# Two raw weight pieces in a free F buffer, and six conversion steps dealt earlier, in a kernel of a recurrent attention and a hardswish layer

## The chip, the cores and the metric

The kernel runs on one core of one Trainium2 chip. The metric is the device time of one execution in microseconds; the time before is the median of three runs. The engines are called PE (TensorE), DVE (VectorE), ACT (ScalarE), POOL (GpSimd) and SP (SyncE, which here only issues DMAs).

## The reference

Four batches of eight heads go through a recurrence of 768 steps with a state of 40 x 40 for each head; its output, 3072 rows of 320, goes through two dense layers with a hardswish between them. The inputs of the recurrence are float32. The two weights, 320 x 2048 and 2048 x 320, come as float64.

```python
for t in range(S):
    kt, vt, rt = (k[:, :, t], v[:, :, t], r[:, :, t])
    wt, at, bt = (w[:, :, t], a[:, :, t], b[:, :, t])
    y[:, :, t] = np.einsum('bhd,bhde->bhe', rt, state)
    Sa = np.einsum('bhde,bhe->bhd', state, at)
    state_decay = state * wt[:, :, None, :] - np.einsum('bhd,bhe->bhde', Sa, bt)
    state = state_decay + np.einsum('bhd,bhe->bhde', vt, kt)
x = y.transpose(0, 2, 1, 3).reshape(B * S, H * D)
h = x @ w_in
g = h * np.clip(h + 3.0, 0.0, 6.0) / 6.0
return (g @ w_out).astype(np.float32)
```

## The kernel before, in words

**Units.** The sequence is cut into chunks of 64 steps. A unit is two batches over one chunk (128 partitions), a group is four units (NU), and there are six groups, 24 units. For each unit `prepare` makes what doesn't depend on the state, in stages named W, gam, A, B, F, K, factor, E and EV. Within a chunk the recurrence is a triangular system; `invert` solves it for the four units of a group at once, from the tile F that the units' F stages have filled, and `third_block` (called X and Y in the plan for the first group) finishes it. `step` then does what depends on the state, in stages RT, VT, C, R, U, UT, S, rS, sn, H, y, move and move2. Most stages put matmuls into a PSUM tile that rotates over a few buffers (`ps_pair`), and then take the result out with DVE or ACT: y writes yg (L977, for the first two units) or ys (L980, which POOL then turns into yg, L981); sn adds to the state (L954); C, E and H take a masked score (L517); UT, S, RT, VT and rS are taken out by ACT (L917, L880, L831, L864, L933). The stages move and move2 send yg to xt, the input of the dense layers, by eight DMAs on SP (L995, L1000); move2 fills the third slot of xt, which only the narrow last part of the features uses.

**Dense layers.** `feed_forward` yields matmuls in small pieces: `expand` makes h (L1051), takes it out by a relu on ACT (L1066) and a multiply on DVE (L1067) into gt, and `contract` multiplies gt by wout (L1092). `pieces(n)` puts n of them into the order. The two PSUM buffers of h are shared by successive jobs. The first job takes unit 0, the second unit 1.

**Weights.** The float64 weights are loaded raw, as pairs of 32-bit words, in 20 pieces of 512 KB, and converted on the chip. `load_weights` is a generator: each `next` is one step, and a piece takes four of them. The first masks the high words into `parts` (DVE, L349) and turns the exponent into a factor by two ACT instructions (L350, L352); the second multiplies the piece before (DVE, L360); the third and fourth make the mantissa (DVE, L369 and L373). Raw pieces need a home in SBUF, and `raw_homes` names one for each piece: a to h are parts of a tile `raw` with tag F (a, b), of wout and win (c to f) and of tinv (g, h); "x", "fb" and "tt" are buffers of `invert`. `free` gives the piece that must have been converted before a home may be filled again. A load (DMA on SP, L327) is issued as soon as its home is free and `limit` lets it; `limit` is 13 at first and 20 after the fourth line of the plan. Tag F has two buffers: F of the first group is in one, `raw` in the other.

**Order.** The schedule is manual: each engine runs its instructions in the order in which the program records them, SP its DMAs too. The second half of the first group's work follows a plan written out by hand. An entry such as 3UT:10 runs stage UT of unit 3 and deals 10 conversion steps between its matmuls and what takes their result out. A part of the plan:

```python
0sn:2 0H:1 Y:2
1U 1UT:2 0y
2RT:1 Y:1
1sn:1 1H:1 2VT:2 0move 0move2
1y:2 2R
2S:3 3RT:2
1move 1move2 2U:3 2UT:1 2C:5
3R:4 3VT
2rS:3 2sn:3 2H:4 3S:2
2y:3 3U:1 3UT:10 3C:5
```

With the last of these lines the second group begins: its W is transposed (L471) into `one` and `pair`, ACT copies it out (L534, L538), and DVE runs the scans L541 and L552. Its WA tile, with tag x, is loaded before that.

Of the kernel before, what the change touches and what calls it, by code (L numbers as in the profile page):

```python
# [8 lines left out]
F32 = mybir.dt.float32  # L9
I32 = mybir.dt.int32  # L10
U32 = mybir.dt.uint32
# [5 lines left out]
P = 128  # L17
BL = 64
# [12 lines left out]
def kernel(  # L31
# [50 lines left out]
    NH = NU * H  # L82
# [8 lines left out]
    inv = ctx.enter_context(tc.tile_pool(name="inv", bufs=1))  # L91
# [129 lines left out]
    for i in range(3):  # L221
        t = const.tile([P, H, BL], F32, name=f"score{i}")
# [14 lines left out]
    for p in range(NP):  # L237
        t = const.tile([P, 2, NPR, SLOT], F32, name=f"state{p}")
        nc.vector.memset(t[:], 0.0)
        state.append(t)  # L240
        t = const.tile([P, 2, NPR], F32, name=f"last{p}")
# [16 lines left out]
    for i, (x, y) in enumerate([(0, DFF // 2), (0, NJ // 2)]):  # L258
        for n, z in enumerate((x, y)):
            t = win[:, :, z:z + H * SLOT] if i == 0 else \  # L260
                wout[:, z:z + 4, :].rearrange("p j m -> p (j m)")[:, 0:2 * H * SLOT].rearrange(
                    "p (n x) -> p n x", n=2)
            t = t.rearrange("p n (h e) -> p n h e", e=SLOT)
            name = ("WA", "BK")[i][n]
# [3 lines left out]
    for u in range(2):  # L268
        t = win2[:, u * NPR * P:(u + 1) * NPR * P]
        placed["rgam", 2 + u] = t.rearrange("p (r t) -> p r t", t=P)  # L270
    WC = 256
# [5 lines left out]
    def raw_homes():  # L277


        raws = inv.tile([P, NH, BL], F32, name="raw", tag="F", bufs=2)  # L280
        raws = raws[:].rearrange("p h t -> p (h t)").bitcast(U32)
        places = [raws[:, n * 4 * WC:(n + 1) * 4 * WC] for n in range(2)]
        for j in (NJ // 4, 3 * NJ // 4):
            places.append(wout[:, j:j + NJ // 4, :].rearrange("p j m -> p (j m)")[:, 0:4 * WC].bitcast(U32))
        places = [x.rearrange("p (n c t) -> p n c t", n=2, t=2) for x in places]
        for c in (DFF // 4, 3 * DFF // 4):
            x = win[:, :, c:c + 2 * WC].bitcast(U32)
            places.append(x.rearrange("p n (c t) -> p n c t", t=2))
        x = tinv[:].rearrange("p h t -> p (h t)").bitcast(U32)
        for n in range(2):  # L290
            y = x[:, n * 4 * WC:(n + 1) * 4 * WC]
            places.append(y.rearrange("p (n c t) -> p n c t", n=2, t=2))
        a, b, c, d, e, f, g, h = places
        order = [g, h, a, b, c, d, e, f, a, b, c, d, "x", "fb", "tt", a, b, "fb", "tt", a]
        free = [None] * 8 + [2, 3, 4, 5, None, None, None, 8, 9, 13, 14, 15]
        left = {}
        for n, (x, before) in enumerate(zip(order, free)):
            if isinstance(x, str):
                if x not in left:
                    left[x] = inv.tile([P, L, L], F32, name=f"raw_{x}", tag=x)  # L300
                x = left[x][:].rearrange("p t s -> p (t s)").bitcast(U32)
                x = x.rearrange("p (n c t) -> p n c t", n=2, t=2)
            yield x, before

    def load_weights():
# [3 lines left out]


        todo, homes = weight_pieces(), raw_homes()
        loaded, done, issued = deque(), [], [0]
        upcoming = []
# [843 lines left out]
    third, F, group_F = [], None, []  # L1157
# [65 lines left out]
    n, cleared = 0, []  # L1223
# [19 lines left out]
    def block(i, j):  # L1243

        if i % NU < 2:
            if j == 0:
# [5 lines left out]

    PLAN = """X X:2 0U:4 0UT:2 1R
              0sn:2 0H:1 Y:2
              1U 1UT:2 0y
              2RT:1 Y:1
              1sn:1 1H:1 2VT:2 0move 0move2
              1y:2 2R
              2S:3 3RT:2
              1move 1move2 2U:3 2UT:1 2C:5  # L1260
# [193 lines left out]
```

## Time and profile before

| what | value |
|---|---|
| median of 3 runs | 799.37 us (797.8 to 799.43) |
| profiled execution | 800.17 us |
| its span | 798.4 us, mean granted clock 0.956 |
| 70 to 80 us | PE busy 9.62, DVE 6.63, ACT 8.51 of 10 us |
| 110 to 120 us | PE busy 6.25, DVE 7.19, ACT 4.79 of 10 us |
| 120 to 130 us | PE busy 8.07, DVE 9.64, ACT 4.76 of 10 us |
| 200 to 210 us | PE busy 9.93, DVE 7.44, ACT 6.07 of 10 us |

The span runs from the first to the last instruction of the program; the time of an execution has a little around it. Times inside the profile are counted from the start of the span. A row of a timeline gives start, length, engine, source line, operation, the tile written and those read, shapes and the count of equal instructions in a row, and in brackets how long the engine had been idle before it and what ended that. Line numbers are those of the kernel before.

### The profile page before, as it was taken

To read this page: it belongs to the slowest core of one execution; us is meant where nothing else is said; L and a number is where in the kernel's file an instruction comes from. 1 tells how busy PE (TensorE), PEld (TensorE's weight loads), DVE (VectorE), ACT (ScalarE), POOL (GpSimd) and SP (SyncE) were. 2 spreads that over 40 slices of the span, in tenths; PEclk is the share of its full clock that TensorE was granted. 3 is DMA by queue.
4 is the path that set the end of the run, shared out by engine and by line. 5 is a ranking of instruction groups with operands and counts; after the bars stand their busy time and mean duration, and the time that the engine had idled before them with its cause. 6 is when DMAs were issued, how large, how long until landed. Compare 5 with 4: busy or idle time off the path is not lost.

```text
span 798.4 us, 35296 instructions
## 1 busy us (share of the span) xinstructions
PE 734.0 (92%) x15832; PEld 624.0 (78%) x15832; DVE 500.5 (63%) x986; ACT 307.1 (38%) x648; POOL 177.1 (22%) x318
## 2 busy tenths in 40 slices
PE   5726778999999989999999999999999999999998
PEld 4625667878778878788888888888888888888886
DVE  7898877689546699445798355888444983323210
ACT  2337653222553424452334454334444324412111
POOL 6403012421223313123214123304222202000000
PEclk9855798999999999999999999999999999999999
DMA  9693653420324322233212223213222101110000
GB/s 122 113 202 87 155 140 55 78 46 9 57 51 72 62 44 39 44 62 59 45 40 42 49 54 63 50 30 62 40 51 45 24 16 29 30 25 13 14 19 17
DMA packets 174214, 45.02 MB, mean 56 GB/s; under 512 B 157424, under 2 KB 172784, under 8 KB 174064
## 3 DMA queue, kind: packets, MB, share of 16 engines
q1 hardware_dynamic: 169760, 42.03, 27.8%
q8 instruction: 125, 2.05, 1.1%
q10 hardware_dynamic: 4304, 0.74, 0.7%
q14 instruction: 25, 0.20, 0.1%
HBM read 34.08 MB, written 3.93 MB: 48 GB/s over the span
## 4 chain that ended last, share of the span: by engine, by line
PE 77%; DVE 8%; issue 5%; SPq 5%; DMA 3%; ACT 1%; POOL 1%; POOLq 0%; DVEq 0%; ACTq 0%
PE h L1051 27%; PE o L1092 23%; PE pair L509 4%; PE pair L969 3%; SPq L455 3%; PE one L471 2%; PE pair L946 2%; PE pair L481 2%; PE pair L853 2%; PE pair L891 2%; PE pair L687 1%; PE pair L911 1%; PE pair L927 1%; PE one L875 1%; SPq L452 1%
## 5 line engine op out<-in xcount | busy, mean ns | idle before, releaser
L1051 PE MATMUL h<-xt,win 128*128 128x128 f32 (+1 forms) x2304 | 252.6, 284 | 3.2 <-DVE gt L1067 2.7
L1051 PEld LDWEIGHTS h<-xt,win 128*128 128x128 f32 (+1 forms) x2304 | 232.9, 193 | 20.6 <-issue 5.4
L1092 PE MATMUL o<-wout,gt 128*128 128x320 f32 x768 | 230.2, 443 | 0.0
L1092 PEld LDWEIGHTS o<-wout,gt 128*128 128x128 f32 x768 | 138.3, 190 | 50.2
L1067 DVE SCALAR_TENSOR_TENSOR gt<-gt,h 128x512 f32<-128x512 f32 x96 | 62.0, 682 | 71.2 <-ACT gt L1066 71.0
L1066 ACT ACTIVATE gt<-h,three 128x512 f32<-128x512 f32 x96 | 62.2, 686 | 101.6 <-PE h L1051 101.2
L981 POOL TENSOR_TENSOR yg<-ys,gam 128x512 f32<-128x512 f32 x22 | 39.7, 1803 | 162.6 <-DVE ys L980 71.8
L738 DVE TENSOR_TENSOR prod<-x 128x30 f32<-128x30 f32 (+9 forms) x180 | 67.2, 373 | 8.8 <-POOL x L723 3.3
L660 POOL TENSOR_TENSOR KBt<-K,rgt 128x320 f32<-128x320 f32 x22 | 19.1, 866 | 212.3 <-ACT rgt L649 207.4
L744 DVE TENSOR_TENSOR x<-x,prod 128x30 f32<-128x30 f32 (+9 forms) x180 | 62.3, 346 | 5.4
L954 DVE TENSOR_TENSOR state<-pair,state 40x320 f32<-40x320 f32 (+1 forms) x44 | 21.4, 487 | 65.5 <-PE pair L946 39.2
L517 DVE COPY_PREDICATED score<-mask,pair 128x512 f32<-128x512 int32 x71 | 50.0, 723 | 1.7 <-PE pair L509 1.2
L980 DVE TENSOR_TENSOR ys<-pair,ys 128x512 f32<-128x512 f32 x22 | 15.2, 690 | 40.9 <-PE pair L687 21.7
L552 DVE TENSOR_TENSOR_SCAN wm<-wm,start 128x528 f32<-128x528 f32 x24 | 37.6, 1566 | 0.8
L541 DVE TENSOR_TENSOR_SCAN prods<-wm,start 128x528 f32<-128x528 f32 x24 | 30.1, 1260 | 10.2 <-ACT wm L538 10.1
L831 ACT ACTIVATE RT<-pair 128x512 f32<-128x512 f32 x21 | 12.5, 597 | 52.8 <-PE pair L481 52.7
L692 ACT ACTIVATE EV<-pair 64x320 f32<-64x320 f32 x44 | 19.0, 432 | 33.7 <-PE pair L687 23.1
L806 ACT ACTIVATE tinv<-pair 32x256 f32<-32x256 f32 x48 | 18.0, 375 | 30.1 <-PE pair L796 29.4
L569 POOL COPY gam<-prods 128x256 f32<-128x256 f32 x24 | 22.5, 938 | 30.6 <-DVE prods L541 26.7
L1110 ACT ACTIVATE ob<-o 128x320 f32<-128x320 f32 x22 | 9.6, 435 | 49.4 <-PE o L1092 29.6
L969 PE MATMUL pair<-score,KBt 64*64 64x64 f32 x1472 | 27.4, 221 | 1.1 <-DVE state L954 0.9
L969 PEld LDWEIGHTS pair<-score,KBt 64*64 64x64 f32 x1472 | 24.0, 134 | 3.7 <-DVE state L954 1.4
(262 smaller groups left out, 1061.6 us busy)
## 6 DMA issues: line engine op xcount, KB each, us to landing
V<-in_v_dram SPq DMA_DIRECT2D x96, 40.0 KB
out_dram<-ob SPq DMA_DIRECT2D x47, 80.0 KB
R<-in_r_dram SPq DMA_DIRECT2D x92, 40.0 KB
B<-in_b_dram SPq DMA_DIRECT2D x42, 80.0 KB
K<-in_k_dram SPq DMA_DIRECT2D x42, 80.0 KB
W<-in_w_dram SPq DMA_DIRECT2D x37, 80.0 KB
A<-in_a_dram SPq DMA_DIRECT2D x37, 80.0 KB
xt<-yg SPq DMA_DIRECT2D x72, 40.0 KB
```

The source lines that it names most:

```text
L509: nc.tensor.matmul(out=o[i][half(q), n, :], lhsT=lhs[half(i, D), n ^ (2 * q * swap), half(q)], rhs=rhs[half(i, D), n, half(q)], start=True ...
L517: nc.vector.copy_predicated(out=x[:].rearrange("p (i h) t -> p i h t", i=2), mask=mask8, data=o[2])
L541: nc.vector.tensor_tensor_scan(out=prods[:].rearrange("p r m i -> p (r m i)"), data0=wm[:, 0:SCAN], data1=start[:], initial=0.0, op0=ALU.m ...
L552: nc.vector.tensor_tensor_scan(out=back, data0=back, data1=start[:], initial=0.0, op0=ALU.mult, op1=ALU.add)
L738: nc.vector.tensor_tensor(out=pv, in0=_ap(x[:], (i + 1) * L + i, [[L, n], [0, i]]), in1=_ap(x[:], i * L, [[0, n], [1, i]]), op=ALU.mult,)
L744: nc.vector.tensor_tensor(out=rest, in0=rest, in1=pv, op=ALU.add)
L969: nc.tensor.matmul(out=y[q][half(s), pr, :], lhsT=o[name][half(q), h * D:h * D + SLOT], rhs=m[name][half(q), 4 * rs + 2 * s + j, :], start ...
L981: nc.gpsimd.tensor_tensor(out=yg[:], in0=m["ys"][:].rearrange("p r q t -> p r (q t)"), in1=o["G"][:], op=ALU.mult)
L1051: nc.tensor.matmul(out=hp[c][:, i, :], lhsT=lhsT, rhs=rhs, start=(begun[c] == 0), stop=(begun[c] == 3 * NQ - 1))
L1066: nc.scalar.activation(out=gt[:], in_=hp[c][:], func=AF.Relu, bias=three[:], scale=1.0)
L1067: nc.vector.scalar_tensor_tensor(out=gt[:], in0=gt[:], scalar=6.0, in1=hp[c][:], op0=ALU.min, op1=ALU.mult)
L1092: nc.tensor.matmul(out=op[:], lhsT=gts[c][:, n, :], rhs=wout[:, c * HJ + r * NQ + n, :], start=((split or r == 0) and c == 0 and n == 0), ...
```

## The change

The 16th and 17th piece get a home of their own, a tile `more` with tag F, that is, the buffer of the first group's F, which is no longer needed then; the pieces behind them move up in the list of homes. With that, three pieces (the two in `more`, and the first in a) are issued without waiting for late conversions, and the last home is "fb". In the plan three steps are dealt behind the matmuls of y of unit 0, where there were none, and four instead of one behind those of sn of unit 1; the steps that are dealt later are thereby six steps further on. PE's order of instructions is the same as before. On SP the three loads stand ahead of the moves of unit 0; the load of the 19th piece stands behind them, and that of the last behind the moves of unit 1, ahead of WA.

```diff
-        order = [g, h, a, b, c, d, e, f, a, b, c, d, "x", "fb", "tt", a, b, "fb", "tt", a]
-        free = [None] * 8 + [2, 3, 4, 5, None, None, None, 8, 9, 13, 14, 15]
+        order = [g, h, a, b, c, d, e, f, a, b, c, d, "x", "fb", "tt", 0, 1, a, b, "fb"]
+        free = [None] * 8 + [2, 3, 4, 5, None, None, None, None, None, 8, 9, 13]
         left = {}
         for n, (x, before) in enumerate(zip(order, free)):
+            if isinstance(x, int):
+                if x == 0:
+                    more = inv.tile([P, NH, BL], F32, name="more", tag="F", bufs=2)
+                    more = more[:].rearrange("p h t -> p (h t)").bitcast(U32)
+                x = more[:, x * 4 * WC:(x + 1) * 4 * WC].rearrange("p (n c t) -> p n c t", n=2, t=2)
             if isinstance(x, str):
@@
               0sn:2 0H:1 Y:2
-              1U 1UT:2 0y
+              1U 1UT:2 0y:3
               2RT:1 Y:1
-              1sn:1 1H:1 2VT:2 0move 0move2
+              1sn:4 1H:1 2VT:2 0move 0move2
               1y:2 2R
```

## The prediction

> **What bounds the kernel now.** I read the page's busy times first, then where TensorE (PE) waits, then the stretch from 78 to 135 us on each engine's timeline, then that stretch in windows that follow the clock's own steps.
>
> ```profile
> PE 734.0 (92%) x15832; PEld 624.0 (78%) x15832; DVE 500.5 (63%) x986; ACT 307.1 (38%) x648; POOL 177.1 (22%) x318
> ```
>
> PE is the bound over the whole. In windows of 10 us it is busy for 8.6 to 10 us everywhere from 140 to 790 us, so what an early stage gains can be carried to the end, but only as PE time. The change works between 78 and 122 us, where PE waits. The timelines of DVE, ACT and PE there (start, length, row, idle time before it and its releaser):
>
> ```profile
> 79.92 0.69 DVE L977 TENSOR_TENSOR yg<-lent,gam 128x512 f32<-128x512 f32 x1 [1.97 <-PE lent L969]
> ...
> 84.91 0.49 DVE L954 TENSOR_TENSOR state<-pair,state 128x320 f32<-128x320 f32 x1 [2.62 <-PE pair L946]
> ...
> 111.14 0.43 DVE L349 TENSOR_SCALAR parts<-raw 128x512 uint32<-128x512 uint32 x1 [2.21 <-DMA raw<-in_moe_w_out_dram]
> ...
> 115.24 0.43 DVE L349 TENSOR_SCALAR parts<-raw_fb 128x512 uint32<-128x512 uint32 x1 [1.54 <-DMA raw_fb<-in_moe_w_out_dram]
> ```
>
> ```profile
> 121.25 0.58 ACT L917 ACTIVATE UT<-pair 128x512 f32<-128x512 f32 x1
> ```
>
> ```profile
> 108.39 1.16 PE L1051 MATMUL h<-xt,win 128*128 128x128 f32 x8 [2.06 <-DVE gt L1067]
> ...
> 113.16 0.69 PE L911 MATMUL pair<-tinv,RR 64*64 64x64 f32 x32 [2.07 <-DVE ys L980]
> ...
> 121.93 1.08 PE L471 MATMUL pair<-ident,WA 128*128 128x128 f32 x4 [3.60 <-issue]
> ...
> 131.41 1.34 PE L969 MATMUL pair<-score,KBt 64*64 64x64 f32 x64 [0.87 <-DVE state L954]
> ```
>
> DVE has two holes (1.97 and 2.62 us) early, and later waits twice for raw weight pieces (2.21 and 1.54). Behind those waits stand ys, and on ACT three conversion pairs (L350, L352) ahead of UT. UT ends at 121.83 and the transposes of WA, which need its PSUM pair, start at 121.93: the 3.60 us put down to "issue" are UT's. From there a full DVE (122.83, the first scan L541, to 131.3) sets y of unit 3 at 131.41. The windows (length, busy time of each engine, clock, DMA share, GB/s):
>
> ```profile
> 107.11:110.53 3.42, 2.14 (x80) 2.02 (x82) 1.49 (x3) 1.08 (x2) 0.00 (x0) 1.00 0.76 194
> 110.53:113.94 3.41, 1.34 (x92) 1.22 (x88) 2.56 (x5) 1.77 (x3) 0.70 (x1) 1.00 0.88 206
> 113.94:117.35 3.41, 3.41 (x41) 3.29 (x31) 2.07 (x5) 1.45 (x2) 0.89 (x1) 0.50 1.01 301
> ...
> 120.77:124.18 3.41, 2.25 (x11) 2.28 (x12) 3.27 (x6) 2.27 (x6) 0.04 (x1) 0.50 0.00 0
> 124.18:127.59 3.41, 3.41 (x55) 2.96 (x57) 3.28 (x6) 0.83 (x2) 3.41 (x6) 0.50 0.52 84
> ...
> 168.55:171.97 3.42, 1.97 (x68) 1.61 (x68) 3.25 (x6) 0.50 (x2) 3.09 (x5) 1.00 0.13 23
> 171.97:175.38 3.41, 3.41 (x40) 2.47 (x39) 3.24 (x10) 1.23 (x3) 0.00 (x0) 0.50 0.47 83
> ```
>
> The granted clock is 1.00 or 0.50 for a whole window. A window with 1.45 us of idle PE (168.55) or 2.07 (110.53) is followed by 0.50, one with 1.28 (107.11) is not; 0.50 ends only behind a full window (124.18, not 120.77).
>
> **The change, part by part.**
>
> *Six steps moved forward.* A piece costs DVE L349 0.42, L360 0.68, L369 0.42 and L373 0.69, 2.2 us, and ACT 0.72 + 0.72. Six steps are a piece and a half: 3.3 us of DVE. The three behind y of unit 0 (L369, L373, L349: 1.53) fit in the hole of 1.97, the three behind sn of unit 1 (L349, L360, L369: 1.52) in that of 2.62. On ACT one pair slips ahead of RT (80.51) and tinv; they end some 0.7 us later, and nothing waits for them. Cost: nothing. Were a hole gone, it would be 1.5 us each. All other DVE rows from 85 to 103 us keep their places, six steps further on.
>
> *Loads.* Pieces 16 to 18 no longer wait for a freed home and are issued behind raw_tt, at 89 us, ahead of unit 0's moves. Three issues of 0.52 put all that SP does behind them (moves, R, WA) 1.6 us later, and 1.5 MB stand ahead of the moves in the DMA queues. Before, DMA is nearly idle there (28 GB/s from 93.46 to 96.87); at the rate of 317 GB/s from 98 to 99 us the 1.5 MB take 4.7 us from about 92.3, to 97.0. PE comes to unit 0's first h at 97.17. The trace shows no landing times, so bounds: nothing, if the moves pass the loads, to 1.3 us, if they land at 98.5. I take 0.5, below the middle: the loads' last byte is due about when PE comes to h. The last three moves serve the narrow part of h alone, at 105 us. The Trainium skill, "DMA: Bandwidth & Descriptors", Queues, rings and completion order, says that an engine takes its ring's descriptors in order, which speaks against this change; without that rule the term would be 0.
>
> *A worse place on ACT.* With the pieces six steps on, ys of unit 2 (L933, before 102.19) comes behind one more pair: L349 ends at 101.7, the pair at 103.2, ys at 103.8, 1.0 later, and H waits for its PSUM. Behind state (103.2) DVE has L349, L360, L369, L373 (2.0), then the score (0.73) and the L349 of piece 18, to 106.3. Its pair (to 107.9) and S (108.4) now stand straight ahead of the relu L1066: first relu 109.05, first gt 109.7, h of unit 1 at 109.9 instead of 108.39; with the 0.5 of the moves, 110.4. PE idles 2.8 us ahead of it.
>
> *Clock there.* 2.8 us is over every idle sum above that brought 0.50, and I take 0.50: h x8 2.07 (row at 114.46) and y of unit 2 2.12 (row at 77.77) instead of 1.16 each. ys L980 starts at 114.3 instead of 112.41. At 1.00 it would be 112.7.
>
> *The tail.* Here the three DMA waits and two of three ACT pairs are gone; the last piece (raw_fb, issued near 108; the old one took 5.0 us from 110.27 to DVE's release) is there by 113. From ys (0.69): L360, L369, L373, L349, 2.0 with overlaps, to 117.0; pair to 118.5; UT to 119.1; WA transposes at 119.2 instead of 121.93. On DVE the last multiply to 119.2, the score to 119.9, first scan at 119.8: 3.0 earlier than 122.83. Scan to y of unit 3 took 8.6, so y stands at 128.4, 3.0 early.
>
> *What is late next.* PE runs from 119.2 through h, rS, sn, H and o at full clock to about 125.3 and waits 3.1 us for y, instead of 0.87. That brings 0.50 and it lasts through the rest of a window and one full one, some 5.1 us: 2.6 of PE time lost (1.7 to 3.4 for one or two whole windows), in a part where PE is then the bound. The lead of 3.0 shrinks to 0.4. "TensorE: Matmul & The Clock Gate", Why this matters for your kernels, warns of idle gaps over about 3 us; by it the 2.8 us gap would keep the clock, and the sum would be nearer to -2. The trace differs (1.45 us idle sufficed), so the row decides.
>
> **Sum.** The profiled execution took 800.17 (span 798.4 and 1.8 around it), 0.8 above the median. -3.0 + 2.6 = -0.4: 799.8 on its scale, 799.0 against the median of 799.37. A measurement of this kernel can tell about 0.2%, 1.6 us, from no change.
>
> **Rivals.** *The clock holds* at y of unit 2 or falls for one window alone at y of unit 3: the scan is 4.6 early (1.6 more) and 1.7 is given back, -2.9, or 3.0 less 1.3 or nothing: 796.4 to 797.7, say 796.5. For it: 107.11 kept 1.00 with 1.28 us idle, and a gap can be split by a window's edge. Against: two gaps near 3 us. *The moves land late*: at the 194 to 206 GB/s of 107 to 114 us the 1.5 MB take 7.5 us, to 99.8, and h starts near 100.5. PE idles 3 us more, at 0.50; state of unit 2, the relu and the whole DVE tail come 2.5 to 3.3 later, the lead of 3.0 is gone and the clock's loss stays: +2.3 (between 1.6 and 3.0), 801.7. It decides from a landing after 98.6. For it: the queue was at 0.76 to 1.01 share in those windows; against: 317 GB/s for the same kind of piece alone. *The waits only change place* (the last L349 still waits for raw_fb): it would have to land 4 us later than I reckon; the time is 799.4.
>
> **How the numbers follow.** Forecast 0.42, waits unchanged 0.03 (both within 0.2%): 0.45. Clock holds: 0.26. Moves late: 0.29. The range reaches from inside the first rival to the second's price, 797.0 to 801.8; the forecast's own range is 797.8 to 800.9.
>
> **What would show it.** Right: no DVE wait at L349 for raw or raw_fb; relu of unit 0 (106.93 before) near 109; WA transposes near 119; y of unit 3 near 128.5 behind some 3 us of idle PE; 0.50 in the window around it. Wrong: h of unit 0 later than 99 (second rival), a clock of 1.00 from 127 on with y before 129 (first), L349 waits that remain (third).

## The result, and the profile after

The changed kernel is slower. Its median is 801.42 us (797.49 to 805.62, 22 runs) against 799.21 us (796.76 to 801.13, 22 runs) for the kernel before: ratio 1.0027, 95% interval 1.0017 to 1.0038, that is 2.2 us. This is the second rival of the prediction, in its size (801.7) and in its sign; its mechanism is only a part of what happened.

The execution that was profiled took 805.42 us (span 803.7), 4.0 above its median, so the spans (803.7 and 798.4) must not be subtracted. It was also 0.92 us late before the change acts: the first yg starts at 80.84 instead of 79.92. Below, "from yg" means a time counted from the start of that row in its own profile. Line numbers of the kernels after are five higher from the list of homes on (L349 is now L354, and so on). Ratios are turned into us by 799.

The busy times of the whole span hardly differ:

```profile
PE 736.1 (92%) x15832; PEld 625.3 (78%) x15832; DVE 500.6 (62%) x986; ACT 306.9 (38%) x648; POOL 176.2 (22%) x318
```

DVE's timeline after. The holes ahead of yg and of state of unit 1 are filled, as forecast (1.97 to 0.45, 2.62 to 0.66). No masking step waits for a raw piece any more. But one conversion step behind ys takes 1.51 instead of 0.42 us:

```profile
80.84 0.69 DVE L982 TENSOR_TENSOR yg<-lent,gam 128x512 f32<-128x512 f32 x1 [0.45 <-PE lent L974]
...
85.54 0.49 DVE L959 TENSOR_TENSOR state<-pair,state 128x320 f32<-128x320 f32 x1 [0.66 <-PE pair L951]
...
117.47 0.69 DVE L985 TENSOR_TENSOR ys<-pair,ys 128x512 f32<-128x512 f32 x1 [2.11 <-PE pair L974]
118.08 0.68 DVE L365 TENSOR_TENSOR wout<-raw,parts 128x512 f32<-128x512 f32 x1
118.68 1.51 DVE L374 TENSOR_SCALAR raw<-raw 128x512 uint32<-128x512 uint32 x1
```

PE's timeline after, the rows that answer to those of before:

```profile
99.60 5.42 PE L1056 MATMUL h<-xt,win 128*128 128x128 f32 x24 [1.00 <-ACT parts L357]
...
113.41 2.08 PE L1056 MATMUL h<-xt,win 128*128 128x128 f32 x8 [3.60 <-DVE gt L1072]
...
123.35 0.63 PE L476 MATMUL pair<-ident,WA 128*128 128x128 f32 x4 [1.40 <-issue]
...
132.84 1.99 PE L974 MATMUL pair<-score,KBt 64*64 64x64 f32 x64 [3.07 <-DVE state L959]
134.75 4.50 PE L1097 MATMUL o<-wout,gt 128*128 128x320 f32 x8
```

The first h of unit 0 now waits for its input. The releaser in that row is a wrong guess: the semaphores of unit 0's first four moves are complete at 98.90, 99.10, 99.28 and 99.46 (read from the trace's semaphore updates), before 92.7 to 93.65. From yg the h is 1.5 late. 1.00 of that is this wait. The other 0.5 is PE's own delay: on ACT a conversion pair now stands ahead of RT of unit 3, which starts 14.1 from yg in place of 13.0 (ACT before, then after):

```profile
92.91 0.59 ACT L831 ACTIVATE RT<-pair 128x512 f32<-128x512 f32 x1
```

```profile
93.60 0.72 ACT L355 ACTIVATE parts<-parts,low 128x512 f32<-128x512 int32 x1 [0.36 <-DVE parts L354]
94.36 0.72 ACT L357 ACTIVATE parts<-parts,low 128x512 int32<-128x512 f32 x1
94.98 0.58 ACT L836 ACTIVATE RT<-pair 128x512 f32<-128x512 f32 x1
```

Everything behind the h is late in turn, and the clock is 0.50 where PE had waited (length, busy time of each engine, clock, DMA share, GB/s):

```profile
91.24:94.65 3.41, 1.42 (x65) 1.16 (x64) 3.24 (x8) 2.94 (x5) 0.00 (x0) 0.99 0.89 269
94.66:98.07 3.41, 2.46 (x67) 2.38 (x68) 3.34 (x8) 3.22 (x7) 0.00 (x0) 0.50 0.82 266
98.08:101.49 3.41, 2.41 (x12) 2.04 (x11) 3.38 (x7) 2.21 (x4) 0.45 (x2) 0.50 0.24 41
101.50:104.90 3.40, 3.40 (x17) 3.27 (x16) 3.08 (x7) 2.52 (x4) 0.00 (x0) 0.51 0.72 189
...
128.74:132.15 3.41, 1.03 (x4) 0.38 (x2) 3.32 (x9) 0.00 (x0) 0.91 (x4) 1.00 0.34 49
132.16:135.57 3.41, 2.73 (x66) 2.42 (x67) 1.87 (x4) 0.00 (x0) 0.00 (x0) 0.50 0.23 55
135.58:138.98 3.40, 3.40 (x8) 2.12 (x7) 0.11 (x2) 0.00 (x0) 0.00 (x0) 0.50 0.58 93
```

Where the time went, from yg, in us:

| point | before | after | difference | forecast |
|---|---|---|---|---|
| first h of unit 0 | 17.25 | 18.76 | +1.5 | +0.5 |
| state of unit 2 | 23.23 | 25.79 | +2.6 | +0.5 |
| first relu | 27.01 | 31.12 | +4.1 | +2.6 |
| ys of unit 2 | 32.49 | 36.63 | +4.1 | +1.9 |
| first scan of the second group | 42.91 | 43.42 | +0.5 | -3.0 |
| y of unit 3 | 51.49 | 52.00 | +0.5 | -3.0 |
| W's transposes behind the o matmuls | 56.96 | 60.20 | +3.2 | -0.4 |

### The profile page after: what moved, and what is told of

Read it like the earlier page. It is cut to its first block, busy times and chain, and to the rows that moved or that the text cites. A ratio compares the mean times of both kernels' runs of the same rounds, so it can differ in the third digit from the quotient of the medians.

```text
span 803.7 us, 35294 instructions
## 1 busy us (share of the span) xinstructions
PE 736.1 (92%) x15832; PEld 625.3 (78%) x15832; DVE 500.6 (62%) x986; ACT 306.9 (38%) x648; POOL 176.2 (22%) x318
## 4 chain that ended last, share of the span: by engine, by line
PE 76%; DVE 13%; issue 5%; DMA 2%; ACT 2%; POOL 1%; SPq 1%; DVEq 0%; POOLq 0%; ACTq 0%
PE h L1056 26%; PE o L1097 22%; PE pair L514 4%; PE pair L974 3%; PE pair L951 2%; PE one L476 2%; PE pair L486 2%; DVE prod L743 2%; DVE x L749 2%; DVE wm L557 2%; PE pair L896 2%; PE pair L858 1%; DVE prods L546 1%; PE pair L916 1%; PE pair L932 1%
## 5 line engine op out<-in xcount | busy, mean ns | idle before, releaser
L974 PE MATMUL pair<-score,KBt 64*64 64x64 f32 x1472 | 29.2, 230 | 4.6 <-DVE state L959 3.1
L811 ACT ACTIVATE tinv<-pair 32x256 f32<-32x256 f32 x48 | 17.9, 374 | 30.7 <-PE pair L801 30.1
```

The costliest lines, as they stand in the source:

```text
L974: nc.tensor.matmul(out=y[q][half(s), pr, :], lhsT=o[name][half(q), h * D:h * D + SLOT], rhs=m[name][half(q), 4 * rs + 2 * s + j, :], start ...
```

## The experiments

Three causes were put against each other. **L**: the loads ahead of unit 0's moves. **S**: the six steps' new place among ACT's and DVE's work. **C**: the clock, which falls behind PE's wait ahead of y of unit 3 whatever came before. Each ratio is to the kernel before on the same chip. The last column is the time from yg to W's transposes in the profiled execution; it ranks the kernels nearly as the medians do.

| kernel | ratio | 95% interval | W from yg |
|---|---|---|---|
| before | 1 | | 56.96 |
| changed | 1.0027 | 1.0017 to 1.0038 | 60.20 |
| loads_behind | 1.0006 | 0.9996 to 1.0016 | 57.66 |
| homes_only | 1.0004 | 0.9992 to 1.0016 | 58.04 |
| plan_only | 1.0052 | 1.0038 to 1.0066 | 62.17 |
| o_in_gap | 0.9980 | 0.9965 to 0.9995 | 54.35 |
| behind_and_gap | 0.9971 | 0.9960 to 0.9983 | 52.49 |
| behind_gap_pair | 0.9945 | 0.9929 to 0.9961 | 52.60 |
| before_gap | 0.9981 | 0.9970 to 0.9992 | 53.77 |
| loads_on_act | 1.0064 | 1.0052 to 1.0077 | 62.01 |
| moves_on_act | 1.0009 | 0.9995 to 1.0023 | 58.04 |
| pair_only | 0.9991 | 0.9976 to 1.0006 | 56.71 |
| behind_gap_pair_rt | 0.9943 | 0.9923 to 0.9963 | 50.74 |
| h_repeated | 1.0011 | 1.0000 to 1.0022 | 57.26 |

**Loads behind the moves** (loads_behind).

```diff
-        if t == 3:
-            limit[0] = PIECES
+        if t in (3, 4):
+            limit[0] = {3: PIECES - 5, 4: PIECES}[t]
```

> The changed kernel, with one thing put back: pieces 16 to 18 are held until unit 0's eight moves are issued. Theory L (the loads ahead of the moves are the cost): the moves are issued from 89.6 and land by 94; unit 0's first h waits for nothing and starts near 98.0 instead of 99.6; the half clock there is one window shorter; state of unit 2 near 104 instead of 106.6, first relu near 109 instead of 112.0, ys near 114.5 instead of 117.5. Median 799.0 (798.3 to 799.6), 2 to 3 below the changed kernel's 801.4. Theory S (the six steps' new place on ACT and DVE is the cost): no matter, within 0.6 of 801.4. Theory C (the clock's fall ahead of y of unit 3 takes the lead whatever comes before): 0.50 behind 132 remains in any case; under L and C together 799.0.

Measured 1.0006, 1.7 us below the changed kernel (0.5 to 2.8 with both intervals): a little less than L expects (2 to 3), and more than S allows if it were the only cause (0.6). Its PE timeline:

```profile
97.58 4.52 PE L1056 MATMUL h<-xt,win 128*128 128x128 f32 x24
...
129.26 1.99 PE L974 MATMUL pair<-score,KBt 64*64 64x64 f32 x64 [3.06 <-DVE state L959]
131.18 4.41 PE L1097 MATMUL o<-wout,gt 128*128 128x320 f32 x8
```

The moves landed by 94.5 and h waits for nothing, though from yg it is still 0.6 later than before (17.9). State of unit 2 starts at 103.77 and ys at 113.91. From yg, y of unit 3 is 1.9 ahead of before. Behind it the clock is 0.50, and W is 0.7 behind: 2.6 are given back there.

**Homes alone, plan alone** (homes_only, plan_only): one half of the change each.

```diff
 homes_only, against the changed kernel
-              1U 1UT:2 0y:3
+              1U 1UT:2 0y
-              1sn:4 1H:1 2VT:2 0move 0move2
+              1sn:1 1H:1 2VT:2 0move 0move2
 plan_only, against the changed kernel
-        order = [..., "x", "fb", "tt", 0, 1, a, b, "fb"]
-        free = [None] * 8 + [2, 3, 4, 5, None, None, None, None, None, 8, 9, 13]
+        order = [..., "x", "fb", "tt", a, b, "fb", "tt", a]
+        free = [None] * 8 + [2, 3, 4, 5, None, None, None, 8, 9, 13, 14, 15]
```

> The homes of the change with the plan of before: two loads (into more) stand ahead of unit 0's moves, the third behind them; no step is dealt earlier. Theory L: moves land near 97.6, h of unit 0 near 97.9, 0.7 late, and the half clock lasts longer there: 800.0 (799.3 to 800.7). Theory S: nothing has a new place on ACT and two waits for raw pieces go: 798.7 (798.0 to 799.3).

> The plan of the change with the homes of before: six steps dealt earlier, and only one load (16th, 512 KB) ahead of unit 0's moves. Theory L: h of unit 0 at most 0.4 late; the waits for raw pieces at the first masking step come back behind 105; 799.3 (798.7 to 800.2). Theory S: the pairs ahead of ys of unit 2 and ahead of S and relu are there as in the changed kernel, so the cost is too: 801.0 (800.4 to 801.8), first relu later than 109.

homes_only came out at 1.0004, between the two expectations and inside the range of L alone. Its h:

```profile
97.52 5.46 PE L1056 MATMUL h<-xt,win 128*128 128x128 f32 x24 [0.56 <-DMA xt<-yg]
```

Together the runs give a series. Ahead of unit 0's first four moves stand 0, 1, 2 and 3 loads of 512 KB (loads_behind, plan_only, homes_only, changed), and the last of the four is complete at 94.46, 95.95, 97.38 and 99.46, from yg at 14.8, 16.3, 17.7 and 18.6: some 1.3 us for each load. These are single executions: without the two runs that use ACT's queue, the six profiles with no load ahead of the moves have it at 13.1 to 14.8 and the four with three loads at 18.0 to 19.5, so between 1.1 and 2.1 for each. PE is ready for h at 17.1 from yg in plan_only, 17.3 in homes_only and 17.8 in the changed kernel (before 17.25). So the first load is hidden, and h waits 0.56 behind two loads and 1.00 behind three.

plan_only is the slower half, 4.2 us, more than either theory had: L had named the waits for raw pieces, but not their size. With steps six earlier but pieces that still wait for homes, DVE stands 5.15 us at a masking step, ahead of relu's multiply in its order, and PE behind that (DVE's row, then PE's):

```profile
111.70 0.43 DVE L354 TENSOR_SCALAR parts<-raw_fb 128x512 uint32<-128x512 uint32 x1 [5.15 <-DMA raw_fb<-in_moe_w_out_dram]
```

```profile
115.47 2.08 PE L1056 MATMUL h<-xt,win 128*128 128x128 f32 x8 [6.88 <-DVE gt L1072]
```

So the halves don't add (1.0004 and 1.0052 against 1.0027): the homes take away a wait that the plan makes.

**o matmuls into the gap** (o_in_gap); **both remedies** (behind_and_gap); **the same in the kernel before** (before_gap).

```diff
+        owed[0] += {BEGIN + 1: 2, BEGIN + 2: -2}.get(t, 0)
         if t >= BEGIN - 2:
             pieces(3 if t < BEGIN else 1.5 if t < BEGIN + 3 else 0)
```

> The changed kernel, with eight of the profile's o matmuls (2.4 us at full clock) moved from behind y of unit 3 to ahead of it, into the 3.07 us in which PE waits there. Theory C: idle ahead of y of unit 3 falls to 0.7, the clock stays 1.00 through 132 to 139, and the transposes of A come near 134.3 instead of 139.1; 797.0 (796.3 to 798.5). Without C, or if the lead is taken up by a full DVE later on: 801.4 (800.6 to 802.0) though the gap is filled.

> Both remedies at once: loads 16 to 18 behind unit 0's moves, and eight of the profile's o matmuls ahead of y of unit 3. If the two costs are separate they add: measured alone, the first took the ratio to before from 1.0027 to 1.0006 and the second to 0.998, so 0.996, 3.3 us under before: 3.2 below (2.2 to 4.4). First h waits for nothing, y of unit 3 near 128 behind 0.9 us of idle PE at 1.00, A's transposes near 129.5. If the gap's clock gives back whatever was gained ahead of it only in part, or the second half of the loss is one and the same cost: no better than the gap alone, 0.998.

> The kernel before with the same o matmuls ahead of y of unit 3, where PE waits only 0.87 us. Theory C: there is no fall of the clock to avoid in most executions, and 2.4 us of work stand in a gap of 0.9, so y comes 1.5 later, PE has the same work: no change, 1.000 (0.9985 to 1.0015). If the reordering as such is what helped: 0.9955, as much as it did to the changed kernel.

o_in_gap measured 0.9980, 3.8 below the changed kernel, as C expects. PE's timeline of it:

```profile
131.10 1.34 PE L974 MATMUL pair<-score,KBt 64*64 64x64 f32 x64 [0.91 <-DVE state L959]
132.37 0.66 PE L476 MATMUL one<-ident,A 128*128 128x128 f32 x4
```

Both together gave 0.9971, a little less of a gain than the sum of the two (0.9959), whose own uncertainty covers the difference. But the rival's 0.998 lies inside the interval too (up to 0.9983), so this run does not show that the two add. before_gap was a miss: 0.9981 and not 1.000. PE's wait of 0.87 is gone there and work stands in its place; this gain is no matter of the clock, and it was left out of the expectation. It is within the interval of what was measured (0.6 to 2.4 us); whether it is all of it is not shown. So o_in_gap could not settle C by itself: it mixes filled time and clock. That asked for the next run.

**H of unit 3 written four times** (h_repeated): useless work in the gap.

```diff
-            x = scores(m["UT"], m["RT"], swap=True)
+            x = scores(m["UT"], m["RT"], swap=True, times=4 if i == 3 else 1)
...
-        for n in range(NPR):
+        for n in [*range(NPR)] * times:
```

> The changed kernel with the matmuls of H of unit 3 written four times over (the same result, 1.9 us of PE work for nothing), ahead of y of unit 3, in whose 3.07 us of waiting they lie. No work is moved, so a gain can only come from the clock. Theory C: idle ahead of y of unit 3 falls to 1.2, the clock stays 1.00 behind it, y takes 1.34 instead of 1.99 and the o matmuls behind it 2.4 instead of 4.5; 2.7 below the changed kernel where the clock would have fallen, 0.9993 to before (0.9985 to 1.0008). Without C: nothing is gained, 1.0027 (1.0017 to 1.0040).

Measured 1.0011: 1.3 us less than the changed kernel, although PE does some 1.7 us more. The difference of the two ratios, 0.0016, has an interval of about 0.0015 either way, so C holds in sign, and with half of the expected size. In the profile all of it is there:

```profile
131.72 1.34 PE L974 MATMUL pair<-score,KBt 64*64 64x64 f32 x64 [0.91 <-DVE state L959]
132.99 2.42 PE L1097 MATMUL o<-wout,gt 128*128 128x320 f32 x8
```

The profiles agree without exception. In the six kernels with 3.06 or 3.07 us of waiting ahead of y of unit 3 (changed, loads_behind, plan_only, loads_on_act, moves_on_act, pair_only) the clock is 0.50 behind it and the next eight o matmuls take 4.06 to 4.54. In the eight with at most 0.92 it is 1.00; where the eight still stand there (before, homes_only, h_repeated) they take 2.42.

**The pair out of relu's way** (pair_only; behind_gap_pair and behind_gap_pair_rt, both with the loads behind and the o matmuls in the gap as well). The first two deal two steps behind y of unit 2 in place of behind S of unit 3; the third also moves a masking step behind the scaling of the state, so that its pair no longer stands ahead of RT of unit 3.

```diff
-              2rS:3 2sn:3 2H:4 3S:2
-              2y:3 3U:1 3UT:10 3C:5
+              2rS:3 2sn:3 2H:4 3S
+              2y:5 3U:1 3UT:10 3C:5
 only in behind_gap_pair_rt
-              2S:3 3RT:2
-              1move 1move2 2U:3 2UT:1 2C:5
+              2S:3 3RT:1
+              1move 1move2 2U:4 2UT:1 2C:5
```

> The changed kernel with the one masking step and multiply moved from behind S of unit 3 to behind y of unit 2, loads and o where the change has them. Theory S (1.5 to 1.8 us of the loss are the pair ahead of S and relu): relu near 110.3 instead of 112.0, 1.5 below the changed kernel, 1.0008 to before (1.0000 to 1.0018). If the gap ahead of y of unit 3 takes it back: y of unit 3 earlier by 1.5, but the idle ahead of it or the clock's loss grows; 1.0025.

> The kernel with both remedies, and two conversion steps (a masking step with its pair on ACT, and a multiply) moved from behind S of unit 3 to behind y of unit 2, so that this pair no longer stands ahead of S and of the relu of unit 0. Theory S: the relu starts 1.5 to 1.8 earlier, h of unit 1, ys, UT and the transposes of WA with it; 1.5 us below the kernel with both remedies (0.8 to 2.0), 0.994 to before. Rival: the steps are only moved, DVE does them between ys and the first scan, and UT (behind the last pairs on ACT) sets the transposes of WA as before: within 0.6 us of the kernel with both remedies.

> The best kernel so far (loads behind, o in the gap, pair behind y of unit 2) with one more masking step moved behind the scaling of the state, so that its pair on ACT stands behind RT of unit 3 and not ahead of it. Theory S: RT comes 1.4 earlier (its PE wait of 1.9 falls to 0.5), first h near 95.8, and relu, ys and the tail up to 1.4 earlier: 0.993 to before (0.992 to 0.994). Rival: h must wait for the moves' landing near 94.5 no more, but ACT and DVE, full behind it, keep ys and relu where they are: 0.9945.

pair_only measured 0.9991, 2.9 us below the changed kernel (1.4 to 4.3 with both intervals), though its loads are where the change has them and its first h is still later than in the changed kernel (19.6 from yg). More than the pair's 1.5 went: the wait for gt fell from 3.60 to 1.49, the clock stayed at 1.00, and h and y of unit 2 take 1.16 each instead of 2.08 and 1.99. So S holds too, as pair and clock together. PE of pair_only:

```profile
111.28 1.16 PE L1056 MATMUL h<-xt,win 128*128 128x128 f32 x8 [1.49 <-DVE gt L1072]
112.37 1.16 PE L974 MATMUL pair<-score,KBt 64*64 64x64 f32 x64
...
129.42 1.99 PE L974 MATMUL pair<-score,KBt 64*64 64x64 f32 x64 [3.06 <-DVE state L959]
```

behind_gap_pair, with all three remedies, is 0.9945, 4.4 us faster than the kernel before and 2.1 below behind_and_gap, slightly more than expected. It beats both kernels. Against before_gap (0.9981) it is 2.9 faster: that much the change is worth with its loads behind the moves and the pair out of the way.

behind_gap_pair_rt, 0.9943, is no better: its rival came true. RT starts 2.0 earlier (92.13 against 94.13), but UT, with two pairs ahead of it on ACT, starts at 96.38 where it had started at 96.54, and h waits 0.44 for it (97.01 against 97.17).

**Another queue** (loads_on_act, moves_on_act): what makes the moves late, their place in SP's queue or the rate of the DMA engines?

```diff
 loads_on_act
-                nc.sync.dma_start(out=to, in_=src)
+                queue = nc.scalar if 15 < issued[0] < 19 else nc.sync
+                queue.dma_start(out=to, in_=src)
 moves_on_act
-                nc.sync.dma_start(out=dst, in_=src)
+                (nc.scalar if i == 0 else nc.sync).dma_start(out=dst, in_=src)
```

> The changed kernel with the three loads issued on ACT's DMA queue, at the same place of the program, not on SP's. Theory L by the order of a queue: SP's moves have nothing ahead of them, issue from 89.6 and land by 94.5; first h near 97.5 without a wait; median as with the loads behind the moves, 1.0006 to before (0.9995 to 1.002, with 1 to 1.5 us of issuing on ACT). Theory L by bandwidth alone (the DMA engines move 1.5 MB between whatever the queue): moves land with the loads, behind 97, h at 98.5 to 99.6, 1.002 to 1.003.

> The changed kernel with unit 0's first four moves issued on ACT's DMA queue (behind VT, near 90) in place of SP's; the three loads stay on SP where they are. This measures the disputed term of the forecast, what 1.5 MB cost that stand ahead. If the order within the one queue makes the moves late: they land about 2 after their issue, by 93 to 94.5, first h waits for RT and not for xt and starts near 97.6 as with the loads behind the moves; ACT pays 2 to 3 of issuing, which may put S and RT 1 later: 1.0006 to 1.002 to before. If the DMA engines share their rate between queues: landing at 95.5 to 97.5. If the moves wait for the loads in any queue: landing at 98 to 99.5, h at 99.6, 1.0027.

loads_on_act is the slowest of all, and fits neither expectation. ACT's program reaches the first two loads at 80.6, 9 us before SP would, and they then stand against pieces that are needed sooner. SP's issues (start, length):

```profile
86.08 2.58 SPq L333 DMA_DIRECT2D raw_fb<-in_moe_w_in_dram  x2
91.34 1.70 SPq L333 DMA_DIRECT2D raw_tt<-in_moe_w_in_dram  x4
93.14 4.04 SPq L1001 DMA_DIRECT2D xt<-yg  x4
```

raw_tt is issued at 91.3 instead of 87.7 and the moves from 93.1 instead of 91.2. PE besides stands 2.96 us in y of unit 1 for nothing that the profile names, and 2.11 for RT; h of unit 0 starts at 101.45. In moves_on_act the order turned the other way round: ACT issued the moves before SP came to the loads (ACT's queue, then SP's):

```profile
88.34 1.35 ACTq L1000 DMA_DIRECT2D xt<-yg  x1
...
89.73 2.26 ACTq L1000 DMA_DIRECT2D xt<-yg  x3
```

```profile
86.96 4.95 SPq L332 DMA_DIRECT2D raw_tt<-in_moe_w_in_dram  x4
91.95 1.00 SPq L332 DMA_DIRECT2D more<-in_moe_w_out_dram  x2
```

The moves were complete by 94.4, each 2.2 to 3.2 us behind its issue, while SP's queue was still moving raw_fb and raw_tt; h started at 98.08, held by UT and not by xt; 1.0009. That agrees with the Trainium skill, "DMA: Bandwidth & Descriptors", Queues, rings and completion order, which says that an engine takes turns between queues. But the three loads were not ahead of the moves in time, so whether another queue would have passed them, or shared their rate, stays open.

## Why the prediction was wrong

The step that failed is the term for the loads. 0.5 was taken and 1.3 was the upper bound; holding the loads back (loads_behind) is worth 1.7 in the medians, and in the traces state of unit 2 stands 24.1 from yg there against 25.8 in the changed kernel. Two things were wrong in the term.

The first is the landing. The three loads were complete at 95.7, 97.4 and 98.7, the last at 17.9 from yg where the forecast had 17.1 (97.0), and the moves at 18.6, which is about the upper bound (98.5). The rate was not the error. The DMA engines moved 330 GB/s up to 97.0, but the last parts of the loads took 1.7 us more at a low rate (the windows of the changed kernel):

```profile
92.50:97.00 4.50, 1.72 (x57) 1.58 (x60) 4.40 (x11) 3.96 (x8) 0.00 (x0) 0.73 1.01 330
97.00:99.50 2.50, 1.60 (x28) 1.12 (x20) 2.50 (x5) 2.41 (x4) 0.45 (x2) 0.50 0.23 68
```

By the semaphore updates, the sixteen parts of the third load were complete between 96.53 and 98.69, so a rate for the whole queue does not give the end of its last part. Why the last parts were slow is not shown. The working also says that the trace shows no landing times. The same semaphore updates of the profile before do show them: raw_tt, behind which the loads were to stand, was complete at 93.5 there, not by the 92.3 from which the loads were reckoned.

The second is the clock. The wait ahead of the first h keeps it at 0.50 for one window more: 10.2 us in place of 6.8, and the 24 matmuls of h take 5.42 instead of 4.33 (4.52 in loads_behind). The prediction looked for the clock at y of unit 2 and of unit 3 alone.

A second step was wrong as well: that the steps moved forward cost nothing on ACT. It saw the pair ahead of the RT at 80.51, but not the one ahead of RT of unit 3, and PE comes 0.5 later to h. Together, 0.5 beyond the term for the wait, 0.5 for PE's own delay and 1.1 for the clock make state of unit 2 2.6 late, not 0.5.

The worse place on ACT was right in kind: the pair does stand ahead of S and relu and cost 1.5 more by then (2.1 reckoned), the wait for gt was 3.6 (2.8), and the clock fell. 2.9 us went with it in pair_only, against 1.7 in loads_behind and 1.3 in h_repeated; the intervals of the three overlap, so their order is not shown. They sum to more than the loss of 2.2, since the change brings a gain of its own that they hide (2.9, by behind_gap_pair against before_gap).

The tail was sized 1.3 too short: from ys to the first scan 6.8 and not 5.5. 1.1 of it is the one step of 1.51 us. POOL was turning ys into yg meanwhile:

```profile
118.30 1.60 POOL L986 TENSOR_TENSOR yg<-ys,gam 128x512 f32<-128x512 f32 x1 [11.33 <-DVE ys L985]
```

Before, the same POOL row (113.23, 1.59) lay in DVE's wait for raw_fb. No masking step of DVE started beside it: the wait that the change took away stood there.

The sum again: ys is 2.2 later than forecast, 2.1 of it by state of unit 2. (Behind that, the pair cost 0.6 less than reckoned, and from the first relu to h of unit 1 it took 1.45 and not 0.85, so these cancel.) With 1.3 in the tail, the lead of 3.0 is a loss of 0.5. The last term was right: the clock behind y of unit 3 cost 2.7 in the trace (2.6 reckoned). 0.5 and 2.7 are the 3.2 of the trace's table; the medians keep 2.2.

Right, too: both DVE holes hid their steps, all waits for raw pieces went (so the third rival falls), and PE waited 3.07 (3.1) ahead of y of unit 3. The first rival needed a clock that holds there or at y of unit 2; it held at neither in the profile. The second named the loads and the sign. Its limit, a landing after 98.6 (18.7 from yg), was just missed at 18.6, and its slow rate did not come. It had state of unit 2 2.5 to 3.3 late, which came true at 2.6, but by a wait of 1.0, PE's own delay of 0.5 and a window of the clock. That its price is so near to the measured time is in part luck: it has neither the pair ahead of RT nor the slow step in the tail.

## What to carry to other kernels

A load that is let go earlier stands ahead of whatever is issued behind it: before freeing one, look which small transfer with a near due time comes next in that queue, and price the load to the end of its last part, which here came 1.7 us behind the bulk. A wait that is removed uncovers what ran beside it, here a slow step beside POOL and a gap on TensorE that halves its clock. Fill such a gap with work that has no due time: that took 3.8 us off the changed kernel and 1.5 off the kernel before.

## What the runs showed of the hardware

**The clock.** Over the profiles of all fourteen kernels, from 75 us to the end, there are 2843 windows of 3.41 us at 1.00 that another window follows. Of 2763 with at most 1.27 us of idle PE, all but one (1.20, at 214 us in the changed kernel) were followed by 1.00; all 47 with 1.62 or more were followed by 0.50; of 33 between, 26 kept 1.00. 22 of the 55 windows that were followed by 0.50 touch no single gap longer than 2 us, so there is no need of 3 us of idleness in one piece. Of 90 windows at 0.50, 63 were followed by 1.00, none of them with more than 0.46 us of idle PE.

**DVE beside POOL.** A masking step (L374, in loads_on_act L375, in homes_only L354) that starts while POOL's yg runs takes 1.49 to 1.52 instead of 0.42, and ends 0.3 behind it; a multiply of two tiles (L365) that had begun before POOL took its usual 0.68. The Trainium skill, "SBUF — State Buffer", Who interferes with whom, has a port that the two engines lock against each other for a whole instruction, which agrees with this trace.
